# The list that orders a fused attention and feed-forward kernel takes in the attention too, and learns to wait

## The chip, the cores and the metric

The kernel runs on one core of one Trainium2 chip. The metric is the time of one execution on the device in microseconds (us); several runs give a median. One further execution is recorded by the hardware profiler, and every row shown here is from it.

## What is computed

The sizes are N = 6016 tokens, C = 256 channels, F = 2048 hidden units, all float32 (the four weight matrices arrive as float64).

```python
qn = q / (norm(q, axis=1) + 1e-6);  kn = k / (norm(k, axis=1) + 1e-6)   # norms over the tokens
s = kn.T @ qn / tau                     # 256 x 256
a = softmax(s, axis=-1)                 # exp, divided by its row sum + 1e-9
x = v @ a                               # 6016 x 256
x = elu(x @ moe_w_in) @ moe_w_out       # 256 -> 2048 -> 256
return silu(x @ moe2_w_in) @ moe2_w_out # the same sizes
```

## The kernel before

The work has three stages.

**Scores.** q and k are read in 47 rows of 128 tokens each, in 17 chunks (sizes 1, 1, 2, nine times 4, 2, 2, 1, 1, 1) into a ring of 16 rows (`ring`, which shares its place with the later tile `xs`). `scores(i)` multiplies each row in full float32, two matmuls for a row, two passes each. Beside it ACT squares each chunk into one of two buffers of `sums`, and DVE adds it to a running sum in `sums` (L443; L439 halves the sum at the end). `load_ahead` issues the loads on SP, as far ahead as the ring goes. After chunks 1 and 3 the first two weight blocks (`w1i` 0 and 1) are loaded too, and their conversion from float64 is cut into steps (`converted`, a generator) that are called by hand after chunks 4 to 8.

**Norms to softmax.** Four column-sum products in each of two calls (`column_sums`, L423) give the squared norms. The last row's scores follow, then eight loads of the first token group of v, the norms on ACT and DVE (L465 to L477), a product with ones that broadcasts one of them (L480), the transposes of v (L493), the softmax (L503 to L506), the transposes of its exponents (L511) and their split into a hi and a lo part (L514, L515). `warm(n)` puts n products that nobody reads into PE's order, to keep it busy: 10 before the scores, 6, 4 and 2 in this stage. All of this is emitted in the order of the text.

**Two feed-forward layers.** The softmax is folded into the first weight matrix by `m_group` (four of them). The rest goes by token groups of up to 1024 tokens: `x_made` prepares a group (eight loads of v in short runs, a 32x32 transpose on DVE, L215, and hi and lo parts), `first_a` and `first_b` make the hidden units, `second` the output, `y_store` copies it out of PSUM (L765) and stores it. Every product is three matmuls of hi and lo parts (L229). `convert` loads a float64 weight block into one of three buffers `st` and converts it on ACT and DVE: two copies, two tensor_scalar (L209), one scalar_tensor_tensor (L212), one tensor_tensor, and a hi and a lo part (L200, L206).

From `m_group(0)` on the operations are not emitted at once but recorded (`do`), and `in_order` puts them in order: PE keeps the order of the text; for every other engine the list simulates time with the costs of `COST`. An operation's `way` is the longest chain of costs from it to the end. Whenever an engine is free, the ready operation with the longest way goes next. `COST` gives for each engine a fixed cost, a cost per element, a delay until another engine sees the result (`late`) and one until the same engine does (`own`). Each engine then runs its instructions in the order in which they were emitted.

[...] A load on SP that waits for its buffer holds all loads behind it.

Of the kernel before, what the change touches and what calls it, by code (L numbers as in the profile page):

```python
# [30 lines left out]

COST = {
# [3 lines left out]
    "SP": (0.36, 0, 4.0, 4.0),  # L36
# [5 lines left out]
Part = namedtuple("Part", "place turn what")  # L42
Op = namedtuple("Op", "engine cost late own emit reads writes")


def in_order(ops):
# [44 lines left out]
    out = []  # L91
    while any(can.values()):
        at, engine = min((max(free.get(e, 0.0), min(ready[i] for i in c)), e) for e, c in can.items() if c)
        i = max((i for i in can[engine] if ready[i] <= at), key=lambda i: (way[i], -i))
        can[engine].remove(i)
        out.append(i)
        free[engine] = at + ops[i].cost
        for j in after[i]:
            ready[j] = max(ready[j], at + gap(i, j))
            left[j] -= 1  # L100
            if not left[j]:
                can.setdefault(ops[j].engine, set()).add(j)
# [5 lines left out]
def channel_attention_elu_silu(  # L108
# [66 lines left out]
    ops, recording = [], False  # L175

    def do(engine, n, emit, reads, writes, times=1):
        fixed, each, late, own = COST[engine]
        o = Op(
            engine,  # L180
            times * (fixed + each * n),
            late,
            own,
            emit,
            [k for v in reads if isinstance(v, V) for k in v.keys],
            [k for v in writes for k in v.keys],
        )
        if recording:
            ops.append(o)
        else:  # L190
            emit()

    def width(ap):
        n = 1
        for d in ap.shape[1:]:
            n *= d
        return n

    def act(out, src, func, **kw):
        do("ACT", width(out.ap), lambda: nc.scalar.activation(out.ap, src.ap, func, **kw), [src], [out])  # L200
# [4 lines left out]
    def tt(out, a, b, op):  # L205
        do("DVE", width(out.ap), lambda: nc.vector.tensor_tensor(out.ap, a.ap, b.ap, op), [a, b], [out])  # L206

    def ts(out, a, s1, s2, *op):
        do("DVE", width(out.ap) / 2, lambda: nc.vector.tensor_scalar(out.ap, a.ap, s1, s2, *op), [a], [out])  # L209

    def stt(out, a, s, b, op0, op1):
        do("DVE", width(out.ap), lambda: nc.vector.scalar_tensor_tensor(out.ap, a.ap, s, b.ap, op0, op1), [a, b], [out])  # L212

    def turn(out, a):
        do("DVE", width(out.ap), lambda: nc.vector.transpose(out.ap, a.ap), [a], [out])  # L215

    def dma(out, src):
        do("SP", 0, lambda: nc.sync.dma_start(out.ap, src.ap), [src], [out])
# [5 lines left out]
    def product(out, lhs, rhs, start=True, stop=True, **kw):  # L224


        def emit():
            for a, b in ((0, 0), (0, 1), (1, 0)):
                nc.tensor.matmul(  # L229
                    out.ap, lhs[a].ap, rhs[b].ap, start=start and a + b == 0, stop=stop and a == 1, **kw  # L230
                )

        do("PE", width(out.ap), emit, [*lhs, *rhs, *([] if start else [out])], [out], times=3)

# [83 lines left out]
    def converted(name, i):  # L318

# [7 lines left out]
        yield  # L327
# [4 lines left out]
        yield  # L332
# [17 lines left out]
        yield  # L350
# [9 lines left out]
    def convert(name, i):  # L360
        load(name, i)
        for _ in converted(name, i):
            pass

    with tc.manual_schedule():
        make_identity(nc, ident)
        nc.gpsimd.memset(ones, 1.0)
        one_sb, tau_sb, rtau = small[:, 24:25], small[:, 0:1], small[:, 1:2]
# [4 lines left out]
        sq = [sums[:, i] for i in range(2)]  # L373
        acc = sums[:, 2]
        o_c = y_ps[:CT]
# [4 lines left out]
        nch = len(rows)  # L380

        def load_qk(i):
            j, nj = rows[i]
            nc.sync.dma_start(ring[:, 0, j % RJ : j % RJ + nj], qv[:, j : j + nj])
            nc.sync.dma_start(ring[:, 1, j % RJ : j % RJ + nj], kv[:, j : j + nj])

        def scores(i):
            j0, nj = rows[i]
            for j in range(j0, j0 + nj):
                for m in range(CT):  # L390
                    nc.tensor.matmul(  # L391
                        o_c[m][:, :C],
                        ring[:, 1, j % RJ, m * P : (m + 1) * P],
                        ring[:, 0, j % RJ],
# [4 lines left out]
        ahead = 0  # L399

        def load_ahead(j):

            nonlocal ahead
            while ahead < nch and sum(rows[ahead]) <= j + RJ:
                load_qk(ahead)
                ahead += 1

        load_ahead(0)
        nc.sync.dma_start(tau_sb, tau.rearrange("(o a) -> o a", o=1).to_broadcast([P, 1]))
        nc.vector.memset(one_sb, 1.0)  # L410
        nc.scalar.activation(small[:, 25:26], one_sb, AF.Sqrt)
        nc.vector.memset(acc, 0.0)
        nsq = h_ps[0]

        def warm(n):

            for _ in range(n):
                nc.tensor.matmul(nsq[:, C : C + P], ones, ones, start=True, stop=True)

        def column_sums(sums, start, stop):  # L420
            for a in range(2):
                for c in range(CT):
                    nc.tensor.matmul(  # L423
                        nsq[:, a * CT + c : a * CT + c + 1],
                        sums[:, a, c * P : (c + 1) * P],
                        ones[:, 0:1],
# [4 lines left out]

        warm(10)
        early = []
        slots = TJ
        last = nch - 1
        for i, (j0, nj) in enumerate(rows):
            while i > 3 and slots > nj:
                slots //= 2
                nc.vector.tensor_tensor(acc[:, :, :slots], acc[:, :, :slots], acc[:, :, slots : 2 * slots], ALU.add)  # L439
            dst = sq[i % 2]  # L440
            nc.scalar.activation(dst[:, :, :nj], ring[:, :, j0 % RJ : j0 % RJ + nj], AF.Square)  # L441
            if i < last:
                nc.vector.tensor_tensor(acc[:, :, :nj], acc[:, :, :nj], dst[:, :, :nj], ALU.add)  # L443
                scores(i)
            load_ahead(j0 + nj)
            if i in (1, 3):
                load("w1i", i // 2)
                early.append(converted("w1i", i // 2))
            if 4 <= i <= 8:
                for c in early[: i - 3]:  # L450
                    next(c, None)

        column_sums(acc[:, :, 0], True, False)
        column_sums(sq[last % 2][:, :, 0], False, True)
# [4 lines left out]
        for n in range(2):  # L459
            s = slice(n * nj0 // 2, (n + 1) * nj0 // 2)  # L460
            for b in range(4):
                rows_of = vv[: nj0 * P].rearrange("(i b j) c -> b i j c", i=32, b=4)[b]
                nc.sync.dma_start(v0[32 * b : 32 * (b + 1), s], rows_of[:, s])
        x, nr, r, t1, hx = nsq[:, 0:4], small[:, 4:8], small[:, 8:12], small[:, 12:16], small[:, 28:32]
        nc.scalar.activation(nr, x, AF.Sqrt)  # L465
        nc.scalar.activation(small[:, 25:26], one_sb, AF.Exp)
        nc.vector.tensor_scalar(hx, x, 0.5, None, ALU.mult)
        nc.vector.tensor_scalar(nr, nr, 1e-30, None, ALU.max)
        for _ in range(2):
            nc.vector.reciprocal(r, nr)  # L470
            nc.vector.tensor_tensor(t1, hx, r, ALU.mult)
            nc.vector.scalar_tensor_tensor(nr, nr, 0.5, t1, ALU.mult, ALU.add)
        nc.vector.tensor_scalar(nr, nr, 1e-6, None, ALU.add)
        nc.vector.reciprocal(r, nr)
        diag = es.take().ap
        for c in range(CT):
            nc.vector.tensor_scalar(diag[:, c * P : (c + 1) * P], ident, r[:, c : c + 1], None, ALU.mult)  # L477
        warm(6)
        bc_ps = h_ps[1]
        nc.tensor.matmul(bc_ps[:, :C], ones, diag[:, :C], start=True, stop=True)  # L480
        nc.vector.reciprocal(rtau, tau_sb)
        rk = small[:, 16:18]
        nc.vector.tensor_scalar(rk, r[:, CT : 2 * CT], rtau, None, ALU.mult)
        bc = es.take().ap
        nc.scalar.activation(bc[:, :C], bc_ps[:, :C], AF.Copy)

# [3 lines left out]
        def transpose_v0(n):  # L490
            for c in range(CT):
                for j in range(TJ):
                    nc.tensor.transpose(  # L493
                        v_ps[n][c].ap[:, j * P : (j + 1) * P], v0[:, n * TJ + j, c * P : (c + 1) * P], ident
                    )

        transpose_v0(0)
        transpose_v0(1)
        s1 = es.take().ap.rearrange("p (d c) -> p d c", d=CT)
        mx, sm, rs = small[:, 18:20], small[:, 20:22], small[:, 22:24]  # L500
        ex = s1
        for d in range(CT):
            nc.vector.scalar_tensor_tensor(s1[:, d], o_c[d][:, :C], rk[:, d : d + 1], bc[:, :C], ALU.mult, ALU.mult)  # L503
            nc.vector.tensor_reduce(mx[:, d : d + 1], s1[:, d], AX.X, ALU.max)
            nc.vector.tensor_scalar(mx[:, d : d + 1], mx[:, d : d + 1], -1.0, None, ALU.mult)
            nc.scalar.activation(ex[:, d], s1[:, d], AF.Exp, bias=mx[:, d : d + 1], accum_out=sm[:, d : d + 1])  # L506
        warm(4)
        eT_ps = h_ps[1].rearrange("p (c d) -> p c d", c=CT)
        for d in range(CT):
            for c in range(CT):  # L510
                nc.tensor.transpose(eT_ps[:, c, d * P : (d + 1) * P], ex[:, d, c * P : (c + 1) * P], ident)  # L511
# [372 lines left out]
```

## Time and profile before

| | us |
|---|---|
| median of 3 runs | 1079.78 |
| the profiled execution | 1078.04 |
| its span, first to last instruction | 1076.3 |
| PE busy in the span | 1050.3 |
| DVE busy | 850.9 |
| ACT busy | 718.1 |

The span is what the rows lie in: their times run from its start. Busy times are of one engine each and overlap. A matmul's end is modelled, so a busy PE can still be a slow one; the granted clock says whether it was.

### The profile page before, as it was taken

The numbers are of one execution on the slowest core, as the hardware profiler recorded it, in microseconds if no ns is written. First come the engines' busy times: TensorE is split into PE (matmuls) and PEld (weight loads), VectorE is DVE, ScalarE is ACT, GpSimd is POOL, SyncE is SP. The second block draws the span as 40 slices with busy tenths as digits, with TensorE's granted clock in tenths as the row PEclk, the third lists the DMA queues.
The fourth block names the chain that finished last, engine by engine and source line by source line (L and its number), as shares of the span: only waits on it lengthen the run. The fifth ranks groups of instructions, "written<-read, shape, count | busy, mean of one in ns | idle before, by whom it ended". The sixth has DMA issues, their size and how long they took to land.

```text
span 1076.3 us, 13457 instructions
## 1 busy us (share of the span) xinstructions
PE 1050.3 (98%) x4878; PEld 888.7 (83%) x4878; DVE 850.9 (79%) x1433; ACT 718.1 (67%) x1305; POOL 0.8 (0%) x7
## 2 busy tenths in 40 slices
PE   9879999999999999999999999999999999999997
PEld 8767887887888788788898888998888888888997
DVE  5889999879979979988989984757757657657553
ACT  4578997777768668678779864556455556545543
POOL 0000000000000000000000000000000000000000
PEclk9998999999999999999999999999999999999999
DMA  9822225003002002101101501202002002100101
GB/s 342 254 59 79 81 84 150 1 1 68 11 1 49 30 1 35 40 1 40 55 5 59 167 20 40 40 1 69 6 1 67 12 0 62 18 1 17 25 1 40
DMA packets 100178, 54.60 MB, mean 51 GB/s; under 512 B 83088, under 2 KB 84880, under 8 KB 99472
## 3 DMA queue, kind: packets, MB, share of 16 engines
q1 hardware_dynamic: 100112, 53.75, 18.0%
q8 instruction: 38, 0.62, 0.2%
q14 instruction: 28, 0.23, 0.1%
HBM read 41.42 MB, written 12.32 MB: 50 GB/s over the span
## 4 chain that ended last, share of the span: by engine, by line
PE 86%; DVE 6%; ACT 3%; DMA 2%; issue 1%; SPq 1%; DVEq 0%
PE y L229 45%; PE h L229 40%; ACT e L200 2%; DVE sums L443 2%; DVE h L206 1%; DMA st<-in_moe_w_in_dram 1%; ACT gs L200 1%; DMA ring<-in_k_dram 1%; DVE gs L206 1%; DVE e L765 1%; PE y L391 1%; DVE e L212 1%; DMA big<-in_v_dram 0%; ACT xs L200 0%; DVE xs L206 0%
## 5 line engine op out<-in xcount | busy, mean ns | idle before, releaser
L229 PE MATMUL y<-gs,wo 128*128 128x512 f32 (+1 forms) x2112 | 503.8, 387 | 11.1 <-ACT wo L200 6.8
L229 PE MATMUL h<-xs,wa 128*128 128x512 f32 (+1 forms) x1968 | 472.7, 386 | 1.7 <-DVE e L212 1.3
L229 PEld LDWEIGHTS y<-gs,wo 128*128 128x128 f32 x2112 | 396.7, 188 | 89.6 <-DVE e L765 7.9
L229 PEld LDWEIGHTS h<-xs,wa 128*128 128x128 f32 x1968 | 368.5, 188 | 70.8 <-DVE e L212 1.7
L206 DVE TENSOR_TENSOR h<-h,h 128x512 f32<-128x512 f32 (+1 forms) x400 | 269.4, 674 | 86.8 <-PE h L229 78.2
L206 DVE TENSOR_TENSOR gs<-e,gs 128x512 fp32r<-128x512 f32 (+1 forms) x384 | 257.6, 674 | 69.2 <-ACT e L200 65.2
L200 ACT ACTIVATE e<-h 128x512 f32<-128x512 f32 (+1 forms) x384 | 230.2, 601 | 80.8 <-DVE h L206 71.5
L200 ACT ACTIVATE gs<-h 128x512 fp32r<-128x512 f32 (+1 forms) x192 | 117.0, 609 | 150.8 <-DVE h L206 100.1
L212 DVE SCALAR_TENSOR_TENSOR e<-e,h 128x512 f32<-128x512 f32 (+1 forms) x192 | 128.2, 672 | 28.3 <-ACT e L200 28.1
L200 ACT ACTIVATE gs<-e 128x512 fp32r<-128x512 f32 (+1 forms) x192 | 117.0, 614 | 14.2 <-DVE e L212 14.1
L200 ACT ACTIVATE e<-e 128x512 f32<-128x512 f32 (+1 forms) x192 | 117.8, 617 | 2.8
L200 ACT ACTIVATE h<-h 128x512 f32<-128x512 f32 (+1 forms) x80 | 46.3, 579 | 39.2 <-PE h L229 39.0
L206 DVE TENSOR_TENSOR xs<-big,xs 128x512 fp32r<-128x512 f32 (+1 forms) x74 | 48.4, 670 | 5.2 <-ACT xs L200 5.2
L200 ACT ACTIVATE xs<-big 128x512 fp32r<-128x512 f32 (+1 forms) x74 | 43.3, 614 | 12.5 <-DMA big<-yd 9.4
L229 PEld LDWEIGHTS y<-wo,gs 128*128 128x128 f32 x384 | 47.9, 192 | 1.1
L229 PE MATMUL y<-wo,gs 128*128 128x256 f32 x384 | 48.2, 283 | 0.0
L391 PE MATMUL y<-ring 128*128 128x256 f32 x188 | 42.2, 386 | 1.2 <-DMA ring<-in_k_dram 1.2
L391 PEld LDWEIGHTS y<-ring 128*128 128x128 f32 x188 | 36.2, 194 | 6.4 <-issue 1.5
L443 DVE TENSOR_TENSOR sums<-sums 128x2048 f32<-128x2048 f32 (+2 forms) x16 | 27.0, 1691 | 13.3 <-ACT sums L441 12.7
L441 ACT ACTIVATE sums<-ring 128x2048 f32<-128x2048 f32 (+2 forms) x17 | 23.3, 1379 | 13.4 <-DMA ring<-in_k_dram 6.8
L200 ACT ACTIVATE cv<-st 128x512 f32<-128x512 f32 x32 | 21.3, 669 | 10.4 <-DMA st<-in_moe_w_in_dram 8.1
L229 PE MATMUL h<-xs,a 128*128 128x512 f32 x96 | 27.4, 392 | 0.5 <-DVE a L206 0.5
(91 smaller groups left out, 350.8 us busy)
## 6 DMA issues: line engine op xcount, KB each, us to landing
st<-in_moe_w_in_dram SPq DMA_DIRECT2D x16, 512.0 KB, 4.0
st<-in_moe_w_out_dram SPq DMA_DIRECT2D x16, 512.0 KB, 3.5
yd<-e SPq DMA_DIRECT2D x20, 256.0 KB, 2.4
big<-yd SPq DMA_DIRECT2D x5, 1024.0 KB, 4.8
out_dram<-big SPq DMA_DIRECT2D x40, 128.0 KB, 2.8
ring<-in_q_dram SPq DMA_DIRECT2D x9, 512.0 KB, 7.4
ring<-in_k_dram SPq DMA_DIRECT2D x9, 512.0 KB, 8.1
big<-in_v_dram SPq DMA_DIRECT2D x32, 128.0 KB, 3.5
```

What stands on the lines that cost most here:

```text
L200: do("ACT", width(out.ap), lambda: nc.scalar.activation(out.ap, src.ap, func, **kw), [src], [out])
L206: do("DVE", width(out.ap), lambda: nc.vector.tensor_tensor(out.ap, a.ap, b.ap, op), [a, b], [out])
L212: do("DVE", width(out.ap), lambda: nc.vector.scalar_tensor_tensor(out.ap, a.ap, s, b.ap, op0, op1), [a, b], [out])
L229: nc.tensor.matmul(out.ap, lhs[a].ap, rhs[b].ap, start=start and a + b == 0, stop=stop and a == 1, **kw)
L391: nc.tensor.matmul(o_c[m][:, :C], ring[:, 1, j % RJ, m * P : (m + 1) * P], ring[:, 0, j % RJ], start=j == 0, stop=j == NJ - 1,)
L441: nc.scalar.activation(dst[:, :, :nj], ring[:, :, j0 % RJ : j0 % RJ + nj], AF.Square)
L443: nc.vector.tensor_tensor(acc[:, :, :nj], acc[:, :, :nj], dst[:, :, :nj], ALU.add)
L765: do("DVE", m, lambda t=t, y=y: nc.vector.tensor_copy(t.ap, y.ap), [y], [t])
```

## The change

1. Loads, scores, squares and sums, column sums, norms, softmax and transposes are recorded as well, and `in_order` orders everything in one list. `xs`, `gs` and `wa`, which take the places of `ring`, `sums` and `v0`, become `Later` tiles, which are made when the list comes to that point.
2. The conversions of `w1i` 0 and 1 are no longer called by hand in the score loop; they stand in the text just before `m_group(0)`, with their loads.
3. A load's cost on SP goes by its size: 330 kB per us, or 110 kB per us for the loads of v in short runs (`short=True`), and 2.3 us until it has landed; before, each cost 0.36 and 4.0.
4. In the text, the transposes of the first half of v and two warm-ups stand before the broadcast product, in place of six warm-ups; the two warm-ups after the softmax go.
5. `in_order` may now let an engine wait. If an operation with a longer way becomes ready before the chosen one would be done, and its ready time plus its way comes within `WAIT` = 0.5 us of the estimated end (`end`), the list takes the longest-way operation that fits in before it, or else leaves the engine idle until then.

```diff
+SPREAD = 330e3, 110e3
+WAIT = 0.5
 COST = {
...
-    "SP": (0.36, 0, 4.0, 4.0),
+    "SP": (0.37, 0, 2.3, 2.3),
+    "-": (0.0, 0, 0.0, 0.0),
...
-    out = []
+    out, end = [], max(way)
     while any(can.values()):
         at, engine = min((max(free.get(e, 0.0), min(ready[i] for i in c)), e) for e, c in can.items() if c)
         i = max((i for i in can[engine] if ready[i] <= at), key=lambda i: (way[i], -i))
+        next_ = [ready[j] for j in can[engine] if ready[j] > at and way[j] > way[i] and ready[j] + way[j] > end - WAIT]
+        if next_ and min(next_) < at + ops[i].cost:
+            fit = [i for i in can[engine] if ready[i] <= at and at + ops[i].cost <= min(next_)]
+            if not fit:
+                free[engine] = min(next_)
+                continue
+            i = max(fit, key=lambda i: (way[i], -i))
+        end = max(end, at + way[i])
         can[engine].remove(i)
...
+    def dma(out, src, short=False):
+        size = 4 * int(np.prod(out.ap.shape))
+        n = max(1, size / SPREAD[short] / COST["SP"][0])
+        do("SP", 0, lambda: nc.sync.dma_start(at(out), at(src)), [src], [out], times=n)
...
+    def matmul(out, lhs, rhs, start=True, stop=True, **kw):
+        emit = lambda: nc.tensor.matmul(at(out), at(lhs), at(rhs), start=start, stop=stop, **kw)
+        do("PE", max(430, 2 * width(out.ap)), emit, [lhs, rhs, *([] if start else [out])], [out], times=2)
...
-            load_ahead(j0 + nj)
-            if i in (1, 3):
-                load("w1i", i // 2)
-                early.append(converted("w1i", i // 2))
-            if 4 <= i <= 8:
-                for c in early[: i - 3]:
-                    next(c, None)
...
-        warm(6)
-        bc_ps = h_ps[1]
-        nc.tensor.matmul(bc_ps[:, :C], ones, diag[:, :C], start=True, stop=True)
...
+        warm(2)
         transpose_v0(0)
+        bc_ps = V(h_ps[1][:, :C], (("bank", 1),))
+        matmul(bc_ps, V(ones, ()), part(diag, diag.ap[:, :C], 0, 1))
...
-        warm(2)
-        for c in early:
-            for _ in c:
-                pass
-        recording = True
...
+        convert("w1i", 0)
+        convert("w1i", 1)
         m_group(0)
```

## Rows read from the trace of the kernel before

**Rows 1.** The page's table of engines: busy us, share of the span, instructions.

```profile
PE 1050.3 (98%) x4878; PEld 888.7 (83%) x4878; DVE 850.9 (79%) x1433; ACT 718.1 (67%) x1305; POOL 0.8 (0%) x7
```

**Rows 2.** PE's waits, whole span: total us, times, longest us.

```profile
PE y L229 <- ACT wo L200: 6.8, 1, 6.8
PE y L229 <- DVE e L765: 4.0, 6, 0.7
PE h L423 <- DVE sums L443: 3.7, 1, 3.7
...
PE h L229 <- DVE e L212: 1.3, 1, 1.3
```

**Rows 3.** PE in order of time: start us, us, instructions, [idle before, releaser].

```profile
10.73 36.50 PE L391 MATMUL y<-ring 128*128 128x256 f32 x168 [1.17 <-DMA ring<-in_k_dram]
50.89 3.57 PE L423 MATMUL h<-ones,sums 128*128 128x1 f32 x16 [3.66 <-DVE sums L443]
54.32 2.05 PE L391 MATMUL y<-ring 128*128 128x256 f32 x4
...
57.97 0.60 PE L480 MATMUL h<-e,ones 128*128 128x256 f32 x2
58.41 1.04 PE L493 MATMUL y<-ident,v 128*128 128x128 f32 x8
...
63.00 0.50 PE L229 MATMUL h<-wo 128*128 128x512 f32 x1 [0.24 <-ACT wo L514]
...
83.15 5.42 PE L229 MATMUL y<-gs,wo 128*128 128x512 f32 x12 [6.82 <-ACT wo L200]
88.41 2.90 PE L229 MATMUL h<-xs,wo 128*128 128x512 f32 x12
```

**Rows 4.** Stretches after the two long stalls; after POOL stand granted clock, DMA share, GB/s.

```profile
51.00:54.50 3.50, 3.50 (x17) 3.50 (x18) 0.00 (x0) 0.01 (x1) 0.00 (x0) 0.50 0.74 116
...
83.00:85.00 2.00, 1.80 (x3) 1.00 (x4) 2.00 (x5) 1.13 (x3) 0.00 (x0) 0.50 0.76 251
```

**Rows 5.** ACT's waits from 0 to 60 us.

```profile
ACT cv L200 <- DMA st<-in_moe_w_in_dram: 6.2, 2, 3.2
```

**Rows 6.** DVE in order of time.

```profile
29.66 0.88 DVE L209 TENSOR_SCALAR cv<-cv 128x512 f32<-128x512 f32 x2
...
56.67 0.48 DVE L477 TENSOR_SCALAR e<-ident,small 128x128 f32<-128x128 f32 x2
...
64.18 1.29 DVE L206 TENSOR_TENSOR xs<-h,xs 128x512 fp32r<-128x512 f32 x2 [0.24 <-ACT xs L200]
...
78.02 1.23 DVE L215 STREAM_TRANSPOSE big<-big 128x1024 f32<-128x1024 f32 x1
79.18 0.38 DVE L209 TENSOR_SCALAR cv<-cv 128x512 int32<-128x512 int32 x1
79.48 0.68 DVE L206 TENSOR_TENSOR xs<-cv,xs 128x512 fp32r<-128x512 f32 x1
...
177.08 1.25 DVE L215 STREAM_TRANSPOSE big<-big 128x1024 f32<-128x1024 f32 x1 [1.37 <-DMA big<-in_v_dram]
```

**Rows 7.** SP in order of time: start us, us until its last issue was done.

```profile
38.65 0.43 SPq L385 DMA_DIRECT2D ring<-in_k_dram  x1
...
44.42 11.77 SPq L218 DMA_DIRECT2D big<-in_v_dram  x8
71.78 5.21 SPq L218 DMA_DIRECT2D st<-in_moe_w_out_dram  x2
```

**Rows 8.** DMA issues from 34 to 84 us: count, KB each, median us to landing.

```profile
st<-in_moe_w_out_dram SPq DMA_DIRECT2D x2, 512.0 KB, 3.5
...
ring<-in_k_dram SPq DMA_DIRECT2D x3, 128.0 KB, 4.2
```

**Rows 9.** ACT in order of time, before the first w1o block's first copy.

```profile
75.68 1.07 ACT L200 ACTIVATE e<-h 128x512 f32<-128x512 f32 x2
76.64 0.67 ACT L200 ACTIVATE cv<-st 128x512 f32<-128x512 f32 x1
```

**Rows 10.** Stretch 100 to 200 us: PE, PEld, DVE, ACT, POOL busy, granted clock, DMA.

```profile
100.00:200.00 100.00, 97.59 (x428) 79.65 (x427) 97.09 (x175) 87.83 (x162) 0.00 (x0) 1.00 0.33 92
```

## The prediction before the result

> **What bounds the kernel now.** I read the page's table of engines first, because it says which engine can set the time. TensorE is busy for 98% of the span [rows 1], so the whole idle time of PE is about 26 us and no re-ordering can win much more than that. Second comes the table of PE's waits [rows 2], whose largest, beside the start-up, are 6.8, 4.0 (six of them), 3.7 and 1.3 us; with the 1.17 us at 9.56 of rows 3 they make 17 us. All but the six lie in the first 180 us, the stretch that the change touches most. Third comes PE's order of time [rows 3], for the place of each stall and what PE did around it, and fourth the granted clock around the two long stalls [rows 4], because a long stall costs more than its length: PE comes back at 0.50, which is 1.2 GHz of 2.4. After the 3.66 us stall sixteen column-sum passes take 3.57 us, 0.22 each; after the 6.82 us stall twelve product passes take 5.42 us, where the next twelve take 2.90.
>
> So the kernel is four pieces: scores (to 47.2 us, PE without a gap from 10.73 on), the chain from norms to softmax (to 63.0), the start of the first token group (to 88.4), where PE waits for converted weights, and the rest, in which PE hardly waits.
>
> **Part 1: the scores.** The stall at 47.23 (10.73 + 36.50) is a wait for the running sums on DVE [rows 3]. They were late because the first two weight loads were converted inside the score loop, by hand: ACT stood 6.2 us, in two waits, in front of a weight load that had not landed [rows 5], and its squares for the sums queued up behind. DVE also did the two conversions between sums: two tensor_scalar in 0.88 us [rows 6] and three more steps of 0.7, some 2.9 us each. The change takes both conversions out of the loop and lets the list place them. The list gives a ring load a longer way than a weight load (everything up to the softmax hangs on it), and in its model SP is never without a ring load that may go: one row costs SP 0.79 us and PE 0.90, SP starts a ring of 16 rows ahead, and by my count 2.5 us of that lead are left at row 40. So I expect all ring loads first, then the four v loads that PE's program order wants first, then w1i 0 and 1.
>
> Are the sums then in time? A row costs PE 0.869 us (36.50 x 4 / 168). The last load, row 46, needs the slot of row 30, which PE leaves at 10.73 + 27 x 0.869 = 34.2; before it went out at 38.65, and the single rows took 4.2 us to land [rows 7, 8]. So it lands near 38.5, and square and add (0.6 and 0.7 us, an estimate from the smallest steps of the timeline) end by 41. PE arrives at 47.2: the stall goes with 5 us to spare, 3.66 us. The weight loads then go out at about 37 to 38 and land by about 43 (the ring and v loads that are still under way stand in front); two conversions of 2.9 us fill DVE until about 49. That is where the norm chain wants DVE, so the cover is thin: if the loads land 3 us late, the in-order DVE pays up to 3 us. I take 0 and keep 3 in the range. The 1.17 us stall at 9.56 waits for a ring load that left before any weight load, so I leave it (0 to 1.2).
>
> Without the stall PE stays at full clock. The column sums become 16 x 0.13 = 2.1 us (0.13 is a 128-column pass at full clock: eight transposes in 1.04 [rows 3]). What follows is a chain on ACT and DVE: from the end of the column sums (54.46) to the end of both diag steps (56.67 + 0.48 = 57.15) 2.69 us [rows 3, 6]. The broadcast product could have started there, but started at 57.97, behind twelve warm-up passes that had begun late because four passes of the last row took 2.05 us at half clock. After the change PE has the last row (4 x 0.217 = 0.87), two warm-ups (4 x 0.13) and eight transposes (1.04) in the way, 2.4 us, shorter than the chain. So: 47.23 + 2.1 + 2.69 + 0.6 = 52.6 for the end of the broadcast, before 58.57. **Term 1: -6.0 us**, 3.66 of it the stall. Ends: -3 (the conversions in the way) and -7.2 (the stall at 9.56 goes too).
>
> The chain from there to 63.0 is a string of dependent steps on DVE, ACT and PE. Nothing of it is removed; the second half of the transposes stays beside it. I take 0, with 0.7 us (one 128x512 step of DVE in the way) as the far end.
>
> **Part 2: the first group.** PE waits at 76.3 to 83.15 for the conversion of the first w1o block. Its load goes out at 71.78, when the first weight group has freed the buffer, and lands 3.5 us later, at 75.3 [rows 7, 8]. ACT starts the first copy at 76.64, since two steps of another chain stand before it [rows 9]: 1.3 us. Then DVE's five conversion steps depend on one another, and between them the old list put three steps that nobody waited for: a 32x32 transpose of 1.16 us at 78.02, a 0.60 step at 79.48, and one more of 0.60 after the next conversion step [rows 6]. The reason is in the list: a step whose result goes to the same engine is ready only COST's own gap (0.19 us) after its forerunner, and the old rule never waits, so it took a ready step of any length. The new rule waits if the step to come is on the longest way and nothing short enough fits. That is just this pattern, 1.3 + 1.16 + 0.60 + 0.60 = 3.7 us. The buffer order (st) is the same, so the load itself can't go earlier than the group's end. **Term 2: -3.0 us**, since the rule acts only where the model agrees that this chain is the longest. Ends: 0 and, if the shorter stall also spares the clock, 3.7 + 2.5 (5.42 against 2.90) = -6.2. I don't count the clock: 3.8 us of stall would be left, and a stall of 3.66 us was enough to halve it [rows 3, 4].
>
> Where the wait is added, the work that is held back queues up on DVE. It has room, for the lo parts of v (two in 1.29 us [rows 6], so 2.5 for four) and the conversions of w1i 2 and 3 (5.8) can now go into DVE's pauses before 63 us; I count 7 of these 8.3 us.
>
> **Part 3: the rest.** At 177.08 DVE stands 1.37 us before a transpose whose v load has not landed, since the old list priced every load alike; PE loses 1.29 us behind it [rows 2, 6]. The change prices v loads at 1.19 us each on SP; eight took 11.77 us, 1.47 each [rows 7], so the transpose is placed later. **Term 3: -1.3** (0 to -1.3). The L765 waits, 4.0 us in six, are a copy out of PSUM behind other DVE steps; all those steps feed PE, so I see no reason for either sign: 0 (-4.0 to +2).
>
> **Sum.** -6.0 - 3.0 - 1.3 = -10.3 against the profiled execution's 1078.04 (span 1076.3 and 1.74 around it), 1067.7; the median of the runs is 1.74 above that execution, so 1069.5 us. The forecast's own span is -4 to -15: 1065 to 1076.
>
> **Rivals.**
> *Slower: waiting costs DVE more than it gives.* DVE is busy 97% of 100 to 200 us [rows 10], and PE is just fed. A wait of 0.19 us before each dependent step is work pushed back. The first group has 14 conversions with four such gaps, 56 x 0.19 = 10.6 us, and the units between have as many gaps behind ACT. It decides from the point where the waits pass the 2.9 us that are idle there and the 7 us gained before 63: with 20 to 25 us of waits, PE stands 10 to 15 us at the end of the group. That takes term 2 and 3 back and adds to it: -6 + 12 = +6, 1086 us. Against it: the rule asks for a step within 0.5 us of the longest way, and most steps of a PE-bound stretch are not.
> *Less: the first part is given back.* Either the conversions stand in front of the norm chain (+3) or v loads of the next group get in between ring loads. Eight of those hold SP for 11.77 us [rows 7]; a full ring covers 16 x 0.869 = 13.9 us minus the landing, so PE would stand some 4 to 6 us and come back at half clock. The Trainium skill (DMA: Bandwidth & Descriptors, Specifications) wants at least 512 B per transfer for line rate, and these loads go in runs of 128 B; by that rule they would hold up the ring loads behind them too. Sum: -2, 1077.5 us.
> *More: all stalls go.* -6.0 - 6.2 - 1.3 - 4.0 = -17.5: 1062 us.
> *The list comes out as before.* It can't for the front, which was ordered by hand; for the rest it is term 3 and L765 at 0, inside the forecast.
>
> On the clock, the rows show 0.50 after each of the two long stalls. The Trainium skill (TensorE: Matmul & The Clock Gate, Part 1) says that the half clock is the resting state and that activity lifts it; by that rule the six warm-ups that the change drops (6 to 2, 2 to 0) would be missed, and the first weight group (12 passes from 63.0) would run at half clock, 2.7 us more. I expect PE's pauses in the chain to stay under 1 us, as they are now, where the clock held; this belongs to "less".
>
> **How the numbers follow.** Forecast 0.62 (1065 to 1076), less 0.16 (1076 to 1080), more 0.07 (1060 to 1065), slower than before 0.15 (1080 to 1098, a little above). The range 1060 to 1080 leaves out the last one. Faster by over 2% would be under 1058.2 and slower over 1101.4; about 2% is what a measurement of this kernel can tell from no change. All 17 us of stalls, not one left, would be needed with the clock's share on top, so 0.03; the slower rival reaches 1101 only at twice its price, 0.03; within 2% 0.94.
>
> **What will show it.** Right: no PE wait for sums near 47, column sums in about 2.1 us, the broadcast near 52.6, PE's first group product near 57; the w1o stall near 3.8 us with the conversion's DVE steps back to back; no transpose waiting for a v load near 177. Wrong: ACT or DVE standing before a weight load ahead of the norm chain, ring loads with v loads between them, DVE idle for many short times between 60 and 180 with PE waiting at the group's end, or new PE waits after 200 us.

## The result, and the profile after

The changed kernel takes 1064.24 us (median of 4) against 1080.68 of the kernel before: ratio 0.9851, 95% interval 0.9831 to 0.9870, a gain of 1.5%. One of the four executions of the kernel before took 2645.36 us, which nothing here explains, and the ratio leaves it out (the other three: 1079.61 to 1081.58). The profiled execution fell from 1078.04 to 1064.07, its span from 1076.3 to 1062.3: 14.0 us, where -10.3 was forecast. The time lies in the stated range (1060 to 1080) and just below the forecast's own span of 1065 to 1076, in the span that the prediction gave its rival "more" (chance 0.07).

PE's waits after the change, whole span (total us, times, longest us):

```profile
PE h L272 <- DVE small L241: 1.9, 1, 1.9
PE y L272 <- DMA ring<-in_k_dram: 1.9, 1, 1.9
PE h L272 <- POOL ones L414: 1.5, 1, 1.5
PE h L264 <- ACT a L230: 1.2, 1, 1.2
PE y L264 <- ACT wo L230: 1.0, 1, 1.0
```

Against [rows 2] the wait for the sums is gone, the wait for the first w1o block (`wo`, for `y`) fell from 6.8 to 1.0, and the six waits for a copy on DVE went (one of 0.5 for a copy on ACT is left); a new one, 1.9 us for `small`, came. PE in order of time answers to [rows 3] (L272 is now the helper of all scores, warm-ups and sums, L264 that of the products):

```profile
11.06 36.50 PE L272 MATMUL y<-ring 128*128 128x256 f32 x168 [1.86 <-DMA ring<-in_k_dram]
47.40 1.84 PE L272 MATMUL h<-ones,sums 128*128 128x1 f32 x16
49.10 1.11 PE L272 MATMUL y<-ring 128*128 128x256 f32 x4
52.13 0.71 PE L272 MATMUL h<-ones 128*128 128x128 f32 x4 [1.92 <-DVE small L241]
...
54.43 1.22 PE L272 MATMUL h<-e,ones 128*128 128x256 f32 x2
...
60.27 0.51 PE L264 MATMUL h<-wo 128*128 128x512 f32 x1 [0.69 <-ACT wo L230]
...
76.96 3.27 PE L264 MATMUL y<-gs,wo 128*128 128x512 f32 x12 [1.02 <-ACT wo L230]
80.07 2.88 PE L264 MATMUL h<-xs,wo 128*128 128x512 f32 x12
```

The column sums now follow the scores at once and take 1.84 us for 3.57. But the broadcast, forecast to end at 52.6, ends at 55.65 (58.57 before): the gain shrinks from 6 to 2.9 us in between. Then it grows again: the first y product comes at 76.96 (83.15 before), and the second weight group (`h<-xs,wo`) at 80.07 (88.41 before), 8.3 us earlier. The other 5.6 us come after that, where PE is now full. Two stretches follow: the start of the group, with a granted clock of 0.83 (the column behind POOL, as in [rows 4]), and one after it:

```profile
60.00:70.00 10.00, 7.71 (x23) 5.28 (x24) 9.49 (x18) 5.53 (x10) 0.00 (x0) 0.83 0.05 4
200.00:300.00 100.00, 100.00 (x441) 82.17 (x441) 89.96 (x145) 75.00 (x138) 0.00 (x0) 1.00 0.12 28
```

Why the broadcast is late stands in the rows of ACT, in order of time:

```profile
46.82 0.67 ACT L230 ACTIVATE cv<-st 128x512 f32<-128x512 f32 x1 [1.20 <-DMA st<-in_moe_w_in_dram]
...
50.65 0.63 ACT L230 ACTIVATE wo<-cv 128x512 fp32r<-128x512 f32 x1 [2.08 <-DVE cv L238]
51.19 0.15 ACT L230 ACTIVATE small<-h 128x4 f32<-128x4 f32 x1
```

The square root (`small<-h`) could have run when the column sums ended, at 49.24. It stands behind the hi copy of w1i 1 (`wo<-cv`), which waits 2.08 us for DVE's part of that conversion; DVE's own lo part of it (51.31 to 52.00) then stands before the next step of the chain. And the conversion began late, for SP issued the load at 38.61 and it was usable only at 46.82: 8.2 us, where the list reckons 512 KB at 1.59 + 2.3 = 3.9.

### The profile page after: what moved, and what is told of

Same layout as the page of the kernel before. It is cut to its first block, busy times and chain, and to the rows that moved or that the text cites. A ratio compares the mean times of both kernels' runs of the same rounds, so it can differ in the third digit from the quotient of the medians.

```text
span 1062.3 us, 13432 instructions
## 1 busy us (share of the span) xinstructions
PE 1046.0 (98%) x4866; PEld 885.2 (83%) x4866; DVE 851.4 (80%) x1433; ACT 715.4 (67%) x1305; POOL 0.8 (0%) x7
## 4 chain that ended last, share of the span: by engine, by line
PE 92%; DMA 3%; DVE 2%; ACT 1%; issue 1%; SPq 0%; DVEq 0%; ACTq 0%
PE y L264 48%; PE h L264 43%; PE y L272 2%; DMA ring<-in_k_dram 1%; ACT e L230 1%; DMA v<-in_v_dram 1%; DMA small<-in_tau_dram 0%; DMA st<-in_moe_w_in_dram 0%; DVE h L238 0%; SPq L253 0%; DVE e L244 0%; DVE gs L238 0%; DVE cv L244 0%; ACT gs L230 0%; DVE cv L238 0%
## 5 line engine op out<-in xcount | busy, mean ns | idle before, releaser
L264 PE MATMUL y<-gs,wo 128*128 128x512 f32 (+1 forms) x2112 | 500.4, 386 | 1.7 <-ACT wo L230 1.0
L264 PE MATMUL h<-xs,wa 128*128 128x512 f32 (+1 forms) x1968 | 473.9, 387 | 0.0
L264 PEld LDWEIGHTS y<-gs,wo 128*128 128x128 f32 x2112 | 395.8, 188 | 78.0 <-DVE e L828 3.0
L264 PEld LDWEIGHTS h<-xs,wa 128*128 128x128 f32 x1968 | 368.9, 188 | 69.5 <-DVE h L238 2.0
L230 ACT ACTIVATE e<-h 128x512 f32<-128x512 f32 (+2 forms) x385 | 229.7, 600 | 71.7 <-DVE h L238 47.4
L230 ACT ACTIVATE h<-h 128x512 f32<-128x512 f32 (+1 forms) x80 | 46.3, 578 | 38.2 <-PE h L264 38.0
L264 PEld LDWEIGHTS y<-wo,gs 128*128 128x128 f32 x384 | 47.9, 192 | 1.1
L264 PE MATMUL y<-wo,gs 128*128 128x256 f32 x384 | 48.3, 283 | 0.0
L272 PE MATMUL y<-ring 128*128 128x256 f32 x188 | 41.3, 380 | 1.9 <-DMA ring<-in_k_dram 1.9
L272 PEld LDWEIGHTS y<-ring 128*128 128x128 f32 x188 | 35.5, 191 | 6.9 <-issue 2.4
L264 PE MATMUL h<-xs,a 128*128 128x512 f32 x96 | 28.1, 401 | 2.0 <-ACT a L230 1.2
L241 DVE TENSOR_SCALAR cv<-cv 128x512 f32<-128x512 f32 (+1 forms) x64 | 25.9, 424 | 2.1 <-ACT cv L230 2.0
```

The lines of the kernel that those rows point to most:

```text
L230: nc.scalar.activation(at(out), at(src), func, **{k: at(x) for k, x in kw.items()}, **more)
L264: nc.tensor.matmul(at(out), at(lhs[a]), at(rhs[b]), start=start and a + b == 0, stop=stop and a == 1, **kw)
L272: emit = lambda: nc.tensor.matmul(at(out), at(lhs), at(rhs), start=start, stop=stop, **kw)
```

## The experiments

**Which of the three parts did it**, the recording of the front (everything up to the softmax), the waiting rule or the load prices. Six kernels: the changed one without the rule, with the old load prices, without either; and the one before with each of the two alone and with both (its front emitted by hand). The lines that differ; the words behind `#` say in which kernel:

```diff
-WAIT = 0.5
+WAIT = -1e9                            # a_nowait, a_neither
-    "SP": (0.37, 0, 2.3, 2.3),
+    "SP": (0.36, 0, 4.0, 4.0),         # a_oldsp, a_neither
-        n = max(1, size / SPREAD[short] / COST["SP"][0])
+        n = 1                          # a_oldsp, a_neither
```

a_nowait: 

> The changed kernel with the waiting rule off (WAIT = -1e9, so no step ever qualifies); recording and the load prices stay. Theory 1, the rule shortens the first group and also clears the copies out of PSUM: the w1o stall returns to 4 to 6 us with the 1.16 us transpose between the conversion's steps, the L828 waits return (4 us in six), the time is 7 to 9 us above the changed kernel, 1071 to 1073. Theory 2, the copies were late because of the old load prices: the L828 waits stay away and the time is 3 to 5 above, 1067 to 1069. Theory 3, recording the front did it all: within 1 us of the changed kernel.

a_oldsp: 

> The changed kernel with the old price of every load (0.36 us on SP and 4.0 to landing, whatever its size). Theory 1: the front stays within 3 us, since the order of loads by longest way hardly changes; the wait of a transpose for v loads near 177 returns (1.3 us); the copies out of PSUM stay without a stall: 1 to 3 us above the changed kernel. Theory 2: the L828 waits return too, 5 to 7 us above. A third outcome: with every load at 0.36 us the list thinks that SP is mostly free, puts the v loads of the next group between the ring loads, and the scores starve: 5 to 12 us above.

a_neither: 

> The changed kernel with the rule off and the old load prices: only the recording of the front and the new order in its text are left. Theory 1: it keeps the front's gain of 2.7 us up to the first weight product, and what DVE gains from work moved ahead, some 1 to 2 us; 1074 to 1077. If rule and prices were worth nothing it is within 1 us of the changed kernel; if the front alone is worth nothing it equals the kernel before, 1080.

The kernel before with the new lines of `in_order` (b_wait), of `COST` and `dma` (b_sp), or both (b_waitsp):

b_waitsp: 

> The kernel before with the rule and the new load prices, its front emitted by hand as it was. Theory 1: scores to softmax as before (the first weight product at 63.0), the w1o stall 3 us shorter, no L765 waits and no transpose waiting near 177: 8 to 9 us under the kernel before, 1071 to 1072. If the gain of the first group comes from work moved ahead of it by the recording, and not from the rule, this kernel gains only 5 to 6: 1074 to 1075.

b_wait: 

> The kernel before with the waiting rule alone (front by hand, old load prices). The rule is what shortens the first group and clears the copies out of PSUM: the w1o stall falls from 6.8 us to 1 to 3, the L765-type waits are gone or under 1 us together, the transpose near 177 still waits for its v load: 7 to 10 us under the kernel before. If instead the rule needs the new prices to act, the six L765-type waits stay and it is under 4.

b_sp: 

> The kernel before with the new load prices alone (front by hand, no rule). If the prices are worth only the transpose that waited for a v load near 177, 1 to 2 us under the kernel before, with the w1o stall near 6.8 and the six waits of the copies as they were. If the prices carry the gain of the first group, 4 us or more.

Medians, ratios to the kernel before on the same chip (1078.8 us beside all but the changed one), and four stretches of each profiled execution, cut at PE rows: start of the column sums, first product of the first weight group (63.00 in [rows 3]), of the second (88.41), and of the last 72 products. Into the first stretch the clock near 10 us enters too (last section).

| kernel | us | ratio, interval | to sums | sums to group 1 | group 1 to 2 | to the last 72 |
|---|---|---|---|---|---|---|
| before | 1080.68 | 1 | 50.9 | 12.1 | 25.4 | 973.4 |
| b_sp | 1075.52 | 0.9970, 0.9958 to 0.9981 | 52.4 | 12.1 | 25.5 | 969.3 |
| b_wait | 1068.34 | 0.9906, 0.9891 to 0.9921 | 51.7 | 10.8 | 19.9 | 967.8 |
| b_waitsp | 1068.02 | 0.9898, 0.9870 to 0.9925 | 50.9 | 13.3 | 20.1 | 968.3 |
| after | 1064.24 | 0.9851, 0.9831 to 0.9870 | 47.4 | 12.9 | 19.8 | 967.8 |
| a_nowait | 1074.27 | 0.9961, 0.9947 to 0.9975 | 47.0 | 16.9 | 24.0 | 969.5 |
| a_oldsp | 1089.71 | 1.0107, 1.0085 to 1.0128 | 69.7 | 12.6 | 21.9 | 969.4 |
| a_neither | 1096.01 | 1.0166, 1.0145 to 1.0187 | 69.5 | 14.8 | 23.3 | 972.5 |

*The rule* is worth 10 us in the kernel before (b_wait) and 10 in the changed one (a_nowait; 12 by the ratios), 7.5 where the prices are already there (b_waitsp beside b_sp) and 6 with a recorded front and the old prices (a_oldsp beside a_neither). With the front emitted by hand it takes 5.5 us from the first group and 5.5 from the rest: PE's waits of b_wait hold a w1o wait of 2.3 us and one copy wait of 0.6, with the old prices.

```profile
PE y L238 <- ACT wo L209: 2.3, 1, 2.3
...
PE y L238 <- DVE e L774: 0.6, 1, 0.6
```

The copy waits on DVE follow the rule alone: the four kernels without it have five or six (2.3 to 4.0 us), the four with it at most one (0.6 or less), whatever the prices and the front.

With the recorded front the rule is needed one stage earlier too, which I had not foreseen. DVE in order of time in a_nowait, inside the norm chain:

```profile
53.17 0.43 DVE L241 TENSOR_SCALAR cv<-cv 128x512 f32<-128x512 f32 x1 [0.90 <-ACT cv L230]
53.51 0.15 DVE L244 SCALAR_TENSOR_TENSOR small<-small 128x4 f32<-128x4 f32 x1
53.63 0.43 DVE L241 TENSOR_SCALAR cv<-cv 128x512 int32<-128x512 int32 x1
53.97 0.17 DVE L503 RECIPROCAL small<-small 128x4 f32<-128x4 f32 x1
54.09 0.69 DVE L244 SCALAR_TENSOR_TENSOR cv<-st,cv 128x512 int32<-128x512 int32 x1
54.70 0.15 DVE L238 TENSOR_TENSOR small<-small 128x4 f32<-128x4 f32 x1
```

Between the chain's 0.16 us steps (`small<-small`) the list put a ready step of 0.4 to 0.7, so that PE waited 4.0 us for the diag steps; the w1o wait was back at 5.2 and six copy waits at 2.9. That is 4.1 us in the second stretch and 4.2 in the third against the changed kernel.

*The recording* is worth 4 us by the medians and 5 by the ratios on top of the other two (after beside b_waitsp; the intervals just touch). In the profiles 3.5 us lie before the column sums, where b_waitsp waits 3.3 us for the sums. With the prices and no rule it can't be told from nothing (a_nowait beside b_sp).

*The prices* are worth 3 us alone, nothing that can be measured on top of the rule (1068.02 beside 1068.34), and 25 us once the front is recorded: a_oldsp is slower than the kernel before. SP in order of time shows why:

```profile
7.16 4.15 SPq L253 DMA_DIRECT2D v<-in_v_dram  x4
12.25 0.40 SPq L253 DMA_DIRECT2D st<-in_moe_w_in_dram  x1
13.51 5.30 SPq L253 DMA_DIRECT2D v<-in_v_dram  x4
...
23.59 9.57 SPq L253 DMA_DIRECT2D big<-in_v_dram  x7
33.27 0.94 SPq L253 DMA_DIRECT2D ring<-in_q_dram  x1
```

With every load at 0.36 us SP is idle in the model and lets the sixteen v loads of the first two groups go between the ring loads. PE starves and comes back at a lower clock, 0.61 from 30.39 to 36.3 and 0.50 from 39 to 45:

```profile
30.39 5.96 PE L272 MATMUL y<-ring 128*128 128x256 f32 x16 [8.67 <-DMA ring<-in_k_dram]
39.39 25.82 PE L272 MATMUL y<-ring 128*128 128x256 f32 x104 [3.04 <-DMA ring<-in_k_dram]
```

Sixteen passes take 5.96 us there and 3.65 in the changed kernel. I had this outcome at 5 to 12 us above the changed kernel, not 25; it also leaves the sums late again (4.5 us). It is also why a_neither, which I had at 1074 to 1077, took 1096. The forecasts of the other four kernels had the right direction and were 0.4 to 3 us too small; in b_wait the wait near 177, which was to stay, is gone too. Which half of the price matters was tried with the old landing time alone:

```diff
-    "SP": (0.37, 0, 2.3, 2.3),
+    "SP": (0.37, 0, 4.0, 4.0),
```

a_late4: 

> The changed kernel with the prices by size kept and the old 4.0 us to landing. a_oldsp changed both and lost 25 us, with v loads between the ring loads. If the size did that (0.36 us for 512 KB leaves SP idle in the model), the ring loads stay together but for one weight load among them, and the time is within 3 us of the changed kernel. If the landing time did it, 1075 or more.

1063.79 us, ratio 0.9860 (0.9841 to 0.9879): no difference from the changed kernel. So the size did it.

**What the late square root costs.** Four changes to the changed kernel; g_vnorms has those of f_norms and g_v together. The diff is abridged.

```diff
+        norms = ("r",) if (name, i) == ("w1i", 1) else ()
-        copy(w, V(f32(high.ap), high.keys), scale=2.0**-112)
+        copy(w, V(f32(high.ap), high.keys + norms), scale=2.0**-112)   # f_norms; low likewise
+        # g_hold: also ("sm1",) for w1i 2 and 3
-                dma(V(v0[32 * b : 32 * (b + 1), s], (("v", n, b),)), V(rows_of[:, s], ()))
+                dma(V(v0[32 * b : 32 * (b + 1), s], (("v", n, b),)), V(rows_of[:, s], ()), short=True)  # g_v
-        warm(2)
+        warm(2, h_ps[1])                                               # f_warm
```

f_norms: 

> The changed kernel, with one thing more: the two first copies of the conversion of w1i 1 also read the reciprocal norms, so that the list can't put this conversion before the norm chain. Theory 1, the conversion stood in front of the square root on ACT and DVE and cost the chain 2 us, and the clock with it: the square root starts right after the column sums (near 49.3), the broadcast ends near 52.6, the clock holds, and the first weight product moves from 60.3 to 57 or 58; 2 to 4 us under the changed kernel. Theory 2, that time isn't on the path, since the first weight group then waits for the same conversion or the w1o load: within 1 us of the changed kernel.

1065.53 us, 0.9881 (0.9864 to 0.9898). The square root came at 49.65 and the broadcast ended at 53.07, 2.6 us earlier, and the first weight product at 60.55, no earlier; the time is that of neither theory. ACT in order of time:

```profile
52.32 0.68 ACT L230 ACTIVATE cv<-st 128x512 f32<-128x512 f32 x1 [0.98 <-DMA st<-in_moe_w_in_dram]
...
55.06 0.38 ACT L230 ACTIVATE e<-h 128x256 f32<-128x256 f32 x1
```

The copy of the broadcast (`e<-h`) now stands behind the first copies of w1i 2, which waited 0.98 us for a load that was late in its turn, and those of w1i 1: it starts 2.0 us after the broadcast's end. The same fault, one step on.

g_hold: 

> The kernel with the conversion of w1i 1 after the norms (f_norms), and the first copies of w1i 2 and 3 after the softmax sums as well. In f_norms ACT copied the broadcast 2.0 us after PE had made it, behind a copy of w1i 2 that waited for its load. Theory: that is where the earlier norm chain went. Then the copy starts within 0.6 us of the broadcast's end, the first weight product comes near 58 and the time is 1.5 to 3 us under f_norms, 1062.5 to 1064. Rival: the first group is bound by the conversions anyway, and work pushed behind the softmax comes back at the w1o stall (1.4 us in f_norms, 3 to 4 here): no gain, 1065 to 1067.

1064.89 us, 0.9872 (0.9848 to 0.9895). The copy of the broadcast starts 0.04 us after it and the first weight product comes at 58.52, as the theory has it; the time does not follow, and the w1o wait is 1.42 us and not the rival's 3 to 4. PE shows one place where the gain goes, which neither had:

```profile
56.75 0.93 PE L277 MATMUL h<-ident,e 128*128 128x128 f32 x4 [1.91 <-ACT e L230]
58.52 0.80 PE L264 MATMUL h<-wo 128*128 128x512 f32 x1 [0.83 <-ACT wo L230]
59.30 1.39 PE L264 MATMUL h<-wo,wo 128*128 128x512 f32 x2
```

The twelve passes of the first weight group run at a granted clock of 0.50 (58.5 to 64.5) and take 6.0 us; in the changed kernel they run at 1.00 and take 3.3. f_norms has the same (0.50, 5.9 us).

g_v: 

> The changed kernel with the eight loads of the first v group priced as the short ones (1.19 us each on SP for 0.40), since in the profile four of them took 4.0 us on SP. If the list put the conversion of w1i 1 before the norms because it thought the load in earlier than it is, it now places that hi copy after them by itself: the square root follows the column sums within 0.7 us, 1 to 3 us under the changed kernel, 1062 to 1063. If the landing time of the load itself is what it gets wrong, it keeps the copies in front and stays within 1 us.

1063.56 us, 0.9853 (0.9833 to 0.9874). The list moves the hi copy as the theory says: the square root starts 0.04 us after the column sums and the norm chain runs as the prediction had it; the time is within 1 us of the changed kernel all the same. PE:

```profile
51.54 0.70 PE L272 MATMUL h<-e,ones 128*128 128x256 f32 x2 [0.48 <-DVE e L241]
...
56.86 0.50 PE L264 MATMUL h<-wo 128*128 128x512 f32 x1 [0.69 <-ACT wo L230]
...
73.96 4.83 PE L264 MATMUL y<-gs,wo 128*128 128x512 f32 x12 [2.19 <-ACT wo L230]
78.63 2.88 PE L264 MATMUL h<-xs,wo 128*128 128x512 f32 x12
```

The broadcast ends at 52.24 and the first weight product comes 3.4 us earlier than in the changed kernel. The first y product still comes 3.0 us earlier. Of that 1.4 are left at the second group, since the twelve y passes take 4.83 us for 3.27, at a granted clock of 0.58, behind a w1o wait of 2.19 us for 1.02:

```profile
74.00:78.00 4.00, 4.00 (x10) 2.89 (x11) 4.00 (x7) 4.00 (x8) 0.00 (x0) 0.58 0.43 131
```

At 500 us 1.7 are left and at the last 72 products 0.5. The last 1.1 us go without a wait: in the token group of 448-column passes (505 to 565 us) twelve passes take 2.64 us where the changed kernel takes 2.60. f_norms, g_hold and g_vnorms show 2.64 there too, f_warm and a_late4 2.60; why is open.

g_vnorms: 

> f_norms and the v loads priced as short ones together. The list then puts the w1i 2 copies behind the broadcast copy, as g_hold does by force. Same theory: the first weight product near 58, 1062 to 1064; rival as for g_hold: 1065 to 1067.

1064.32 us, 0.9862 (0.9839 to 0.9884). The first weight product comes 10.8 us after the start of the column sums, as in g_hold (12.9 in the changed kernel), and its group runs at a clock of 0.65 (g_v: 0.63).

f_warm: 

> The changed kernel, with the two warm-ups before the transposes of v written to another PSUM bank than the one that holds the squared norms. In the changed kernel they waited 1.9 us for a DVE step that reads that bank. Theory 1: the broadcast waits for the diag steps all the same, so moving this stall gains nothing; PE stands after the transposes instead, and the time is within 1 us of the changed kernel. Theory 2: the stall is on the path or keeps the clock down: 1 to 3 us under it.

1063.84 us, 0.9865 (0.9848 to 0.9881). The warm-ups no longer wait, and PE waits 2.85 us for the diag steps instead, as theory 1 has it; its first weight group runs at 1.00. None of the five can be told from the changed kernel by its interval. So the chain's 3 us are real (g_v), but none of these kernels turns them into time. The traces show three places where they go: late conversion copies (f_norms), a lower clock in the first weight group or behind the w1o wait (f_norms, g_hold, g_v, g_vnorms), and 1.1 us in the 448-column group of the same four. No run takes one of these away alone, so their shares are not shown.

## Why the prediction was right, and where not

The sign, the range and the first stall are right; the sum is 3.7 us short, of terms that missed both ways: +3.1 in term 1, -2.6 in term 2, -4.0 in a term taken as 0. That the total came so close is in part luck.

**Term 1 (-6.0, measured -2.9).** The mechanism was right as far as the sums: no wait near 47, the column sums at full clock in 1.84 us (2.1 forecast). The step that failed is "I take 0 and keep 3 in the range", for the conversions in front of the norm chain: the square root came 1.95 us late behind one of them, and PE stood 1.9 us and made the transposes and the broadcast at a clock of 0.69 over 51 to 56 us. The load behind it was taken to land at 43; the second weight load went out at 38.61, behind four v loads, and landed near 46.8. One of the prediction's signs of being wrong came with it, ACT standing 1.20 us before that load ahead of the norm chain, and the first group product came at 60.27, not near 57. g_v, where the hi copy is out of the way, shows the term as forecast, 52.24 for 52.6.

**Term 2 (-3.0, measured -5.6 from first to second weight group).** Right mechanism; what was left out is the clock. The steps of the first w1o conversion run back to back, the first on ACT, the others on DVE:

```profile
73.05 0.67 ACT L230 ACTIVATE cv<-st 128x512 f32<-128x512 f32 x1
...
73.81 0.88 DVE L241 TENSOR_SCALAR cv<-cv 128x512 f32<-128x512 f32 x2
74.72 0.69 DVE L244 SCALAR_TENSOR_TENSOR cv<-st,cv 128x512 int32<-128x512 int32 x1
75.55 0.69 DVE L238 CUSTOM_DVE_ANT_0 cv<-st,cv 128x1024 uint16<-128x1024 uint16 x1
```

From the first copy to the first y product it now takes 3.9 us for 6.5, and from the first weight product to the first y product 16.7 for 20.2: 3.5 us, near the 3.0 taken. The wait itself fell by 5.8 us, since PE also came to it 2.4 us later, after waits at the group's start and a clock of 0.83 from 60 to 70. The step that failed is "I don't count the clock: 3.8 us of stall would be left": with 1.02 left it held, twelve passes in 3.27 us for 5.42, the other 2.2 us. That the work moved ahead by the recording would pay for it is not borne out: b_wait shortens the group as much with the front by hand.

**Term 3 (-1.3).** The wait that ended at 178.95 is gone. The reason given, the prices, is enough (b_sp), but not needed: the rule alone removes it too (b_wait).

**The L765 waits (0 taken, -4.0 measured).** "I see no reason for either sign" is what failed, and it is as large as the whole missing 3.7 us. The rule that was counted for the w1o chain was not counted here, and it is what removes them: b_wait has one of 0.6 us, a_oldsp too; b_sp keeps five of 2.3. One of the six before, and the same place after:

```profile
265.44 0.68 DVE L765 COPY e<-y 128x512 f32<-128x512 f32 x1
...
267.84 0.68 DVE L765 COPY e<-y 128x512 f32<-128x512 f32 x1
...
268.58 0.96 PE L229 MATMUL y<-gs,wo 128*128 128x512 f32 x3 [0.73 <-DVE e L765]
```

```profile
254.95 0.69 DVE L828 COPY e<-y 128x512 f32<-128x512 f32 x1
...
255.55 0.69 DVE L238 TENSOR_TENSOR gs<-e,gs 128x512 fp32r<-128x512 f32 x1
...
256.34 0.69 DVE L828 COPY e<-y 128x512 f32<-128x512 f32 x1
```

Before, three other steps stand between the two copies, after it one. PE's last products for `y` before the late copy end at 262.7, so on the chip it was ready long before it ran; which choice of the list the rule changed to move it is not shown.

**The rivals.** "Slower", waits that cost DVE its throughput: from 100 to 200 us DVE is busier than before (99%) and PE waits 0.5 us once. "More": the time lies in its span, but not for its reason; not all stalls went (PE's waits still sum to 10 us), and term 1 gave 2.9 of 6.0. "Less" (its 1077.5 should read 1077.8, 1079.78 - 2): the conversions stood in front, as it says; the v loads between ring loads did not occur with these prices, and a_oldsp shows the place and the size they would have: its column sums start at 69.7 for 47.4, 22 us later, where I priced 4 to 6 and the clock. I had bounded them by one ring's cover, but the sixteen v loads and the weight loads emptied it twice (8.67 and 3.04 us).

On the clock: the first weight group did not run at half clock for want of the dropped warm-ups (1.00, 3.3 us), though PE's longest pause before it was 1.92 us and not under 1. It did run at half clock in f_norms and g_hold, which have the same warm-ups, and the price of 2.7 us was right (g_hold). PE's pause before the softmax transposes is longer there (3.85 and 1.91 us for 0.84); whether the dropped warm-ups would have held the clock was not tried.

## What to carry to other kernels

A list that always takes a ready step can pay for every short gap between dependent steps; letting it wait for the step of the longest way was worth some 10 of the 14 to 16 us, with the front recorded or not. Recording more work under a list is only as good as its load prices: with loads that cost SP almost nothing the same list lost 25 us. After that the gain of a chain shows only up to the next thing that is late, or to the next pause that lowers the clock, so follow it to the last wait before counting it.

## What the runs showed of the hardware

The length of a stall alone does not say whether the clock falls. A w1o wait of 2.19 us (g_v) was followed by 0.58 over 74 to 78 us; one of 2.26 in b_wait, which ended at 78.49, by 1.00:

```profile
70.00:80.00 10.00, 7.74 (x33) 5.81 (x32) 9.41 (x19) 9.39 (x18) 0.00 (x0) 1.00 0.24 75
80.00:90.00 10.00, 9.62 (x42) 7.62 (x41) 10.00 (x20) 9.57 (x19) 0.00 (x0) 1.00 0.24 84
```

Near 10 us, where these kernels wait for the same ring load, 1.97 to 2.02 us of waiting was followed by 0.74 to 0.81 over 10 to 15 us (f_warm, g_vnorms, b_wait), 0.84 to 1.86 by 1.00 (g_v, before, after). In the first three the 168 passes behind it take 38.2 us for 36.5. By that and a later start the column sums of f_warm start 2 us later than those of the changed kernel (49.43 for 47.40), though the engines get the same instructions in the same order up to there, so differences of a microsecond between profiled executions of the last experiments are not to be read.
